# Reordering the first loads of a spectral-mixing kernel: filters side by side behind x, weights and the second batch held back

## The chip, the cores and the metric

The kernel runs on one NeuronCore of a Trainium2 chip. The metric is the device time of one execution in microseconds (us), as the median of several runs. "The trace" is the record of one profiled execution; its times count from the start of that execution's span.

## The reference, cut to what matters

```python
def _attn_ref(x, filt_r, filt_i):            # x: (8, 3008, 256), filters: (1505, 256)
    X = np.fft.rfft(x, axis=1)
    Y = X * (filt_r + 1j * filt_i)[None, :, :]
    return np.fft.irfft(Y, n=x.shape[1], axis=1)

def _moe_ref(x, w_in, w_out, beta):          # w_in: (256, 2048), w_out: (2048, 256)
    h = x @ w_in
    g = h * (1.0 / (1.0 + np.exp(-beta * h)))
    return g @ w_out
```

Each of the eight batches is transformed along its 3008 rows, multiplied by a filter, and transformed back. All rows then go through a two-layer network (the FFN).

## The kernel before

The transform is done as small matmuls. The first batch has a stage of its own, about 50 us long, in which little can be overlapped. From the second batch on, the transform of the next batch is hidden under the FFN of the current one. So what matters here is when the first FFN matmul (`hps`) can start.

The first stage needs, in this order: x of batch 0 (forward transform, `first1`), the filters (`product`), and then, for the FFN, w_in, x of batch 1 and w_out. All are loads from memory, issued from two queues:

```python
    x_cur = load_x(0, X_FIRST)                       # POOL queue, six pieces, f32 to bf16
    nc.sync.dma_start(bt[:], ...)                    # SP queue
    mark = dpool.tile([1, D], BF16, name="mark", tag="mark")
    nc.sync.dma_start(mark[:], x_cur[:1, 2 * JG, :]) # SP waits here for x's fifth piece
    ...
    FG = ((0, KG), (KG, KG), (2 * KG, 2 * KG))       # three groups: a quarter, a quarter, a half
    for k0, n in FG:
        load_filter(fr_sb, filt_r, 0, k0, n, nc.sync)   # each: rows upwards, rows downwards
    for k0, n in FG:
        load_filter(fr_sb, filt_i, M, k0, n, gp)        # gp is POOL
    ws = [load_wout(i * WG, WG) for i in range(2)]      # SP, behind filt_r
    ... # five small POOL instructions
    for h in range(WI):
        gp.dma_start(win_sb[:, :, fs], moe_w_in[:, fs]...)   # POOL, behind filt_i
    ... # tables; first1(0) to first1(7) use up x_cur
    xs[1] = load_x(1, X_WHOLE)                       # POOL, into the buffer of x_cur
    ...
    def beta_columns():
        bps = hpsum.tile([P, NFB], F32, name="bps", tag="hps")
        id_f = setup.tile([NFB, NFB], F32, name="id_f", tag="id_f")
        gp.tensor_copy(id_f[:], ident[:NFB, :NFB])   # POOL
        nc.tensor.transpose(bps[:], bt[:], id_f[:])  # TensorE
        nc.vector.tensor_copy(beta_sb[:], bps[:])    # VectorE
    ...
    for i in range(NK // 2 + FLAG):
        if i < NK // 2:
            product(i)        # two matmul pairs, then two VectorE products with fr_sb
        ...
        if i == 3:
            t2_more(1, nc.vector)
            beta_columns()
        ...
        if i >= FLAG:
            inverse3(i - FLAG)
```

`mark` is a copy whose only purpose is to make SP wait: the filt_r loads stand behind it in SP's program and start only when the named piece of x has landed (in the trace the piece landed at 10.78, the mark was issued at 10.80, the first filt_r load at 11.12).

There are twelve pairs of products; `pb_t` and `qb_t` are the two results of a pair. `beta_columns` turns a small vector into columns with a TensorE transpose (`bps`). For it POOL copies `id_f`, a 16x16 unit matrix. The filter's rows upwards are long runs; the rows downwards come as 1 KB pieces (sizes as in the trace's DMA records).

Of the kernel before, what the change touches and what calls it, by code (L numbers as in the profile page):

```python
# [9 lines left out]
P = 128  # L10
# [3 lines left out]
F32 = mybir.dt.float32  # L14
# [10 lines left out]
M = 64  # L25
H = M // 2
NK = 24
J = 32
KG = 6
NG = NK // KG  # L30
JG = 8
# [5 lines left out]
def kernel(  # L37
# [10 lines left out]
    nc = tc.nc  # L48
# [9 lines left out]
    NP = 2 * N1  # L58
# [26 lines left out]
    fr_sb = consts.tile([P, NK, D], F32, name="fr_sb", tag="fr_sb")  # L85
# [17 lines left out]
    def evac(dst, src, on_act, scale=None):  # L103
        if on_act:
            nc.scalar.activation(dst, src, ACT.Copy, scale=1.0 if scale is None else scale)  # L105
        elif scale is None:
            nc.vector.tensor_copy(dst, src)  # L107
        else:
            nc.vector.tensor_scalar_mul(dst, src, scale)  # L109

    def load_x(b, parts):
        t = xpool.tile([NP, J, D], BF16, name="xg", tag="xg")
        xv = x[b].rearrange("(p j) d -> p j d", j=J)
        for p0, p1, j0, j1 in parts:
            nc.gpsimd.dma_start(t[p0:p1, j0:j1, :], xv[p0:p1, j0:j1, :])  # L115
        return t


    X_WHOLE = [(0, 80, 0, J), (80, NP, 0, J)]
    X_FIRST = [(0, 80, 0, JG), (80, NP, 0, JG), (0, 80, JG, 2 * JG), (80, NP, JG, J)]  # L120
    X_FIRST += [(0, 80, g * JG, (g + 1) * JG) for g in range(2, NJG)]

# [29 lines left out]
    setup = sp.enter_context(tc.tile_pool(name="setup", bufs=1))  # L152
# [25 lines left out]
    def warm(n, cols=512):  # L178
        for _ in range(n):
            nc.tensor.matmul(pw[0][:, :cols], lhsT=wz[:, :P], rhs=wz[:, :cols], start=True, stop=True)  # L180
# [4 lines left out]
    nc.gpsimd.iota(ic[:], pattern=[[1, P]], base=0, channel_multiplier=0)  # L185
    x_cur = load_x(0, X_FIRST)
    bt = setup.tile([NFB, P], F32, name="bt", tag="bt")
    nc.sync.dma_start(bt[:], moe_beta.rearrange("(fb fp) -> fb fp", fp=P))

    mark = dpool.tile([1, D], BF16, name="mark", tag="mark")  # L190
    nc.sync.dma_start(mark[:], x_cur[:1, 2 * JG, :])

    gp = nc.gpsimd
    ip_f = small("ip_f")
# [18 lines left out]
    gp.tensor_tensor(keep[:], keep[:], m_p[:], ALU.mult)  # L213
    gp.tensor_scalar(keep[:], keep[:], 0.5, None, ALU.is_gt)

    WI = 2
    for h in range(WI):
        fs = slice(h * FF // WI, (h + 1) * FF // WI)
        gp.dma_start(win_sb[:, :, fs], moe_w_in[:, fs].rearrange("(dc p) f -> p dc f", p=P))
# [84 lines left out]
    def first1(i, on_act):  # L304
        for dc in range(NDC):
            if dc:
                ps = opsum.tile([P, 4, P], F32, name="psa", tag="acc")
            else:
                ps = fpsum.tile([P, 4, P], F32, name="psa", tag="f")
            for e in range(4):  # L310
                nc.tensor.matmul(
                    ps[:, e, :KP],
                    lhsT=x_cur[:, 4 * i + e, dc * P : (dc + 1) * P],
                    rhs=t1b[:],
                    start=True,
                    stop=True,
                )
            evac(
                a_t[:, dc, :, 4 * i : 4 * i + 4, :].rearrange("p k j a -> p j k a"),
                ps[:, :, :KP].rearrange("p j (k a) -> p j k a", a=4),  # L320
                on_act[dc],
            )
# [15 lines left out]
    first1(6, (True, True))  # L338
    warm(2)
    first1(7, (False, True))  # L340
    xs = {}
    if B > 1:
        xs[1] = load_x(1, X_WHOLE)



# [327 lines left out]
    def ux(b):  # L674
        def go():
            xs[b] = load_x(b, X_WHOLE)

# [147 lines left out]
```

## Time and profile before

| what | before |
|---|---|
| time, median of the first three runs | 810.47 us |
| span of the trace | 806.2 us |
| TensorE busy, whole span | 97% |
| VectorE's waits for filt_r | 6.45 and 7.32 us |
| first product, last product (start) | 22.92, 47.84 us |
| first `hps` | 53.19 us |

Busy time by stretches of ten us; the columns are the stretch, its length, busy us (and count) of TensorE, of its weight loads, of VectorE, ScalarE and POOL, then the granted TensorE clock, the DMA engines' busy share (it passes 1 where packets overlap, as with the 1.13 here) and GB/s:

```profile
20.00:30.00 10.00, 5.74 (x53) 5.08 (x53) 6.97 (x15) 4.97 (x9) 0.59 (x3) 0.66 1.13 235
30.00:40.00 10.00, 4.99 (x72) 4.51 (x70) 2.42 (x5) 5.69 (x9) 0.34 (x2) 0.95 1.02 213
40.00:50.00 10.00, 7.64 (x76) 6.49 (x76) 7.80 (x14) 3.85 (x8) 7.24 (x8) 0.70 0.26 80
```

No compute engine is full there, and the granted clock drops to a mean of 0.66 and 0.70 in two of the stretches, but the DMA engines are full until 40 us (1.13 and 1.02). The waits from 10 to 60 us (total, times, longest) name the reason:

```profile
DVE pb_t L424 <- DMA fr_sb<-in_filt_r_dram: 13.8, 2, 7.3
PE ps2q L415 <- DVE qb_t L424: 11.5, 2, 6.2
```

The first line is the cause and the second its echo: TensorE waits for buffers that VectorE has not read. VectorE's timeline gives the two places (start, length, instruction, and in brackets the idle time before it and what ended it), TensorE's timeline the first FFN matmul:

```profile
22.92 0.69 DVE L424 TENSOR_TENSOR pb_t<-ps,fr_sb 128x512 bf16<-128x512 f32 x1 [6.45 <-DMA fr_sb<-in_filt_r_dram]
...
39.87 0.69 DVE L424 TENSOR_TENSOR pb_t<-ps,fr_sb 128x512 bf16<-128x512 f32 x1 [7.32 <-DMA fr_sb<-in_filt_r_dram]
...
47.84 0.68 DVE L424 TENSOR_TENSOR qb_t<-ps2q,fr_sb 128x512 bf16<-128x512 f32 x1
...
53.19 1.02 PE L747 MATMUL hps<-y,win_sb 128*128 128x512 bf16 x4
```

From the first to the last product 24.92 us pass; without the second wait, 17.60. When the loads were issued, from the timelines of the SP and POOL queues:

```profile
10.80 0.27 SPq L191 DMA_DIRECT2D mark<-xg  x1
11.12 0.33 SPq L127 DMA_DIRECT2D fr_sb<-in_filt_r_dram  x1
...
12.43 1.56 POOL L219 DMA_DIRECT2D win_sb<-in_moe_w_in_dram  x2
18.37 1.11 POOL L115 DMA_DIRECT2D xg<-in_x_dram  x2 [4.38 <-PE pb L371]
19.47 0.19 POOL L389 CAST id_f<-ident 16x16 f32<-16x16 bf16 x1
```

So w_in and the second batch are issued 27 and 21 us before filt_r's last group lands (39.8), and share the engines with it: from 28 to 34 us their queue moved 83 packets and filt_r's 83.

### The profile page before, as it was taken

What the parts mean: (1) busy time and instruction counts of PE and PEld (TensorE: products, weight loads), DVE (VectorE), ACT (ScalarE), POOL (GpSimd) and SP (SyncE); (2) the same over time, 40 slices, a digit from 0 to 9 for tenths busy, and PEclk for the clock granted to TensorE, in tenths of its full rate; (3) what the DMA queues carried; (4) which work ended last, traced back from release to release, by engine and by line L of the source; (5) the groups of instructions that cost most, each with busy time, mean ns of one, the idle gap of its engine ahead of it and who ended that gap; (6) DMA issues with size and microseconds to landing.
All of it is one profiled execution on the core that took longest, in us unless ns stands there. A gap on an engine that the chain in (4) does not pass through costs nothing.

```text
span 806.2 us, 15374 instructions
## 1 busy us (share of the span) xinstructions
PE 780.4 (97%) x6101; PEld 550.8 (68%) x6101; DVE 398.7 (49%) x644; ACT 599.1 (74%) x920; POOL 142.2 (18%) x146
## 2 busy tenths in 40 slices
PE   7589999999999999999999999999999999999997
PEld 4466766766667766777667766787666776776665
DVE  6474964565636745275553746446463670500100
ACT  6557787787677876778667886678767788677776
POOL 6070430231002400033001320023100240000000
PEclk9889999999999999999999999999999999999999
DMA  8949379412941249311781118701291124110101
GB/s 182 225 109 221 119 163 216 148 67 100 206 151 42 96 113 193 122 57 67 177 201 59 51 62 208 202 27 69 102 229 47 48 90 111 41 53 28 53 27 52
DMA packets 84209, 91.43 MB, mean 113 GB/s; under 512 B 3563, under 2 KB 75004, under 8 KB 83338
## 3 DMA queue, kind: packets, MB, share of 16 engines
q1 hardware_dynamic: 79930, 72.11, 30.2%
q0 software_dynamic: 2272, 14.94, 9.8%
q10 hardware_dynamic: 1936, 3.41, 2.0%
q8 instruction: 47, 0.77, 0.4%
q14 instruction: 24, 0.20, 0.1%
HBM read 57.16 MB, written 46.66 MB: 129 GB/s over the span
## 4 chain that ended last, share of the span: by engine, by line
PE 88%; DMA 5%; DVE 3%; issue 2%; ACT 1%; POOL 0%; SPq 0%; ACTq 0%; DVEq 0%; POOLq 0%
PE acc L775 39%; PE hps L747 38%; DMA fr_sb<-in_filt_r_dram 3%; PE ps L550 3%; PE ps L498 2%; PE ps L572 2%; PE ps L599 2%; DVE ost L107 1%; DMA d<-a 1%; DMA xg<-in_x_dram 1%; DVE p_t L582 0%; ACT gT L756 0%; DMA a<-d 0%; DVE q_t L583 0%; DVE q_t L586 0%
## 5 line engine op out<-in xcount | busy, mean ns | idle before, releaser
L756 ACT ACTIVATE gT<-hps,beta_sb 128x512 bf16<-128x512 f32 x752 | 516.7, 687 | 177.6 <-PE hps L747 168.5
L775 PE MATMUL acc<-wout_sb,gT 128*128 128x256 bf16 x3008 | 455.1, 272 | 1.5 <-DVE ost L107 0.3
L747 PE MATMUL hps<-y,win_sb 128*128 128x512 bf16 (+7 forms) x1728 | 447.6, 351 | 0.0
L775 PEld LDWEIGHTS <-gT 128*128 128x128 bf16 x3008 | 285.7, 98 | 132.5 <-issue 4.2
L747 PEld LDWEIGHTS <-win_sb 128*128 128x128 bf16 x1728 | 164.8, 98 | 24.8 <-issue 0.5
L589 POOL TENSOR_TENSOR v_t<-p_t,q_t 128x512 bf16<-128x512 f32 x84 | 106.6, 1269 | 379.1 <-DVE q_t L586 371.6
L107 DVE COPY ost<-acc 128x512 f32<-128x512 f32 x87 | 56.1, 683 | 195.7 <-PE acc L775 189.1
L107 DVE CAST a<-ps 96x512 bf16<-96x512 f32 x96 | 65.9, 686 | 84.4 <-PE ps L550 82.8
L109 DVE TENSOR_SCALAR y<-ps 128x376 bf16<-128x376 f32 x118 | 64.4, 548 | 61.6 <-PE ps L498 61.4
L582 DVE TENSOR_TENSOR p_t<-ps,fr_sb 128x512 f32<-128x512 f32 x84 | 58.1, 691 | 33.3 <-PE ps L572 31.9
L586 DVE TENSOR_TENSOR q_t<-ps,fi_sb 64x512 f32<-64x512 f32 x84 | 58.2, 693 | 1.2
L583 DVE SCALAR_TENSOR_TENSOR q_t<-ps,fi_sb 64x512 f32<-64x512 f32 x84 | 57.4, 683 | 1.1
L498 PEld LDWEIGHTS <-zz 96*128 96x128 bf16 x512 | 35.5, 98 | 29.6 <-DVE q_t L586 0.8
L105 ACT ACTIVATE z<-ps 128x512 bf16<-128x512 f32 x84 | 49.5, 590 | 0.6 <-PE hps L747 0.4
L550 PE MATMUL ps<-xg,t 94*96 94x512 bf16 x112 | 41.9, 381 | 0.8 <-DVE a L107 0.7
L498 PE MATMUL ps<-t,zz 96*128 96x94 bf16 x448 | 36.8, 205 | 0.0
L572 PE MATMUL ps<-a,t 128*128 128x256 bf16 x168 | 32.1, 273 | 1.0 <-DMA a<-d 1.0
L599 PE MATMUL ps<-v_t,t 128*128 128x256 bf16 x168 | 32.1, 273 | 0.3 <-DVE q_t L586 0.2
L115 POOL DMA_DIRECT2D xg<-in_x_dram x20 | 10.9, 550 | 121.2 <-PE acc L775 97.7
L572 PEld LDWEIGHTS <-t 128*128 128x128 bf16 x168 | 15.9, 98 | 15.9 <-issue 1.3
L550 PEld LDWEIGHTS <-t 94*96 94x96 bf16 x112 | 13.8, 123 | 13.0 <-issue 1.3
L599 PEld LDWEIGHTS <-t 128*128 128x128 bf16 x168 | 15.4, 98 | 8.1 <-DVE q_t L586 0.5
(112 smaller groups left out, 207.5 us busy)
## 6 DMA issues: line engine op xcount, KB each, us to landing
out_dram<-ost SPq DMA_DIRECT2D x40, 512.0 KB, 2.9
d<-a SPq DMA_DIRECT2D x28, 384.0 KB, 11.1
a<-d SPq DMA_DIRECT2D x28, 384.0 KB, 4.3
d<-z SPq DMA_DIRECT2D x28, 384.0 KB, 3.4
zz<-d SPq DMA_DIRECT2D x28, 384.0 KB, 6.6
xg<-in_x_dram POOLq DMA_DIRECT2D x7, 1280.0 KB, 10.4
out_dram<-ost SPq DMA_DIRECT2D x20, 128.0 KB, 2.4
ws<-in_moe_w_out_dram SPq DMA_DIRECT2D x4, 512.0 KB
```

The costliest lines, as they stand in the source:

```text
L107: nc.vector.tensor_copy(dst, src)
L109: nc.vector.tensor_scalar_mul(dst, src, scale)
L498: nc.tensor.matmul(ps[:, e, :NP], lhsT=zz[:, jj + e, dc * P : (dc + 1) * P], rhs=tab[:], start=True, stop=True,)
L550: nc.tensor.matmul(ps[:KP], lhsT=t1[:], rhs=s["x"][:, 2 * i : 2 * i + 2, :], start=True, stop=True)
L572: nc.tensor.matmul(ps[:, e, :], lhsT=t2[:, k0 + e, 3:5, :].rearrange("p c k -> p (c k)"), rhs=s["a2"][g][:, kk + e, :], start=True, stop=True,
L582: nc.vector.tensor_tensor(p_t[:], ps[:], fr_sb[:, k0 : k0 + 2, :], ALU.mult)
L586: nc.vector.tensor_tensor(q_t[:M], ps[M:P], fi_sb[M:P, k0 : k0 + 2, :], ALU.mult)
L589: nc.gpsimd.tensor_tensor(v_t[:], p_t[:], q_t[:], ALU.add)
L599: nc.tensor.matmul(ps[:, e, :], lhsT=t3[:, k0 + e, :], rhs=v_t[:, e, :], start=True, stop=True)
L747: nc.tensor.matmul(hps[:, pos - t0 : pos - t0 + ln], lhsT=win_sb[:, dc, fb * P : (fb + 1) * P], rhs=ys[b][:, dc, n0 : n0 + ln], start=(dc ...
L756: nc.scalar.activation(gT[:, :tn], hps[:, :tn], ACT.Silu, scale=beta_sb[:, fb : fb + 1])
L775: nc.tensor.matmul(acc[tb // 2][:, tb % 2, :], lhsT=gT[:, tb * P : (tb + 1) * P], rhs=wout_sb[:, fb, :], start=(fb == 0 and tb % 2 == 0), ...
```

## The change

Its intent: order the loads by need. Both filters should come side by side close behind x, and w_in and the second batch only when the first half of both filters has landed. The whole diff:

```diff
+    X_HALVES = [(0, 80, 0, J // 2), (80, NP, 0, J // 2), (0, 80, J // 2, J), (80, NP, J // 2, J)]
...
-    nc.sync.dma_start(mark[:], x_cur[:1, 2 * JG, :])
+    nc.sync.dma_start(mark[:], x_cur[:1, JG, :])
...
+    held = setup.tile([P, 1], F32, name="held", tag="held")
+    for p0 in (H, M + H):
+        gp.tensor_copy(held[p0 : p0 + H], fr_sb[p0 : p0 + H, 2 * KG - 1, :1])
     WI = 2
     for h in range(WI):          # the w_in loads on POOL
...
-        xs[1] = load_x(1, X_WHOLE)
+        xs[1] = load_x(1, X_HALVES)
```

It has three parts: the mark waits for x's third piece instead of the fifth ("the earlier mark"); two tiny POOL copies read the second group of both filters and thereby hold POOL until these have landed ("the hold"); and the second batch comes in four pieces instead of two ("the halves").

## The prediction

> **What bounds the kernel now.** TensorE is busy 97% of the span (page, part 1), but not in the first 50 us: in 20-30, 30-40 and 40-50 us it is busy 5.7, 5.0 and 7.6 of 10 (busy time by stretches), with its clock granted at half for 22.1-28.9 and 39.0-46.0. This first-batch stage is set by VectorE's 24 filter products (pb_t, qb_t, 0.68 us each). VectorE waits for DMA fr_sb<-in_filt_r_dram twice, 13.8 us in all (waits): 6.45 us before the first product (22.92) and 7.32 us before the seventh pair (39.87). The products end at 48.5; the first FFN matmul (hps) starts at 53.2.
>
> Why filt_r is late: its queue (SP) starts only when the mark copy sees x's fifth piece (10.8), and its first packets move at about 16.5. Landings by semaphore: third x piece 8.5, fifth 10.9; filt_i groups 14.1, 16.0, 20.3; filt_r groups 22.9, 26.7, 39.9. The last group took 11 us more because it shared the engines with w_in and with the second batch. From 28 to 36 us the DMA records show 16 KB packets (1.23 us) and 1 KB packets (0.07 us) nearly one for one, so the filter got 0.16 MB in 8 us against 1.39 MB.[...]
>
> **What the change does.**
> 1. mark waits for x's third piece: SP's filter issue moves from 11.1 to about 8.8. filt_r then shares with the end of x and with filt_i.
> 2. Two tiny POOL copies (about 0.2 us each) wait for the second groups of both filters. POOL issues w_in (two issues, 0.78 us each) and the second batch behind them, so they move from 12.4 and 18.4 to about 23 and 24.5. The last filter group then meets only a tail of w_in's 2 KB packets.
> 3. The second batch comes in four pieces with 8 KB packets, 0.55 us of POOL per issue.
>
> No arithmetic moves. DMA is already full from 4 to 39 us, so total load time is conserved: w_out and batch 2 should still land near 41-42.
>
> **Cost on the critical path** (estimates from the above). First filter group lands at about 19 instead of 22.9: -3.9. The products then need 18.3 us of VectorE time with its small waits (25.6 less 7.32). Group 2 is in time, and the third lands near 29, before its need: -7.3. New wait, +2: beta_columns' id_f copy on POOL now stands behind the hold and six issues, about 27 instead of 19.5; the bps transpose and beta_sb (VectorE, in order) would like it at about 25. Products end near 39.5, hps starts near 44. Batch 2 and w_out land just in time, and the rest, TensorE at 97%, shifts as a block. Saving about 9 us, off 810.5.
>
> **Prediction:** 801.3 us, range 797.5 to 805. Faster by over 2%: 0.03; within 2%: 0.95; slower: 0.02.
>
> **What would show it.** VectorE's wait before the first pb_t about 2.5 us, before the seventh pair under 1 us; a new wait of about 2 us at beta_sb or bps, released by POOL id_f; hps at 42-46.
>
> **What would make it wrong.** filt_r no sooner despite the earlier issue; POOL held longer, so the id_f wait reaches 4 us; w_out's 1 KB packets starved by batch 2 until after 44, which would stall the first acc matmuls; x's last pieces delayed enough to push the first stage.

## The result, and the profile after

| what | before | after |
|---|---|---|
| time, median | 809.76 us (4 runs) | 801.85 us (4 runs) |
| ratio | | 0.990 (95%: 0.9878 to 0.9922) |
| span of the trace | 806.2 us | 800.1 us |
| first wait of VectorE for filt_r | 6.45 us | 4.51 us |
| second wait | 7.32 us | none |
| first product, last product (start) | 22.92, 47.84 | 20.79, 41.84 |
| first `hps` | 53.19 us | 47.20 us |

A ratio is the mean time of one kernel's fast runs over that of the other's of the same rounds, so it is not quite the ratio of the medians. A second set of runs, later, gave 802.05 against 808.38 us, ratio 0.9924. The saving is therefore 6 to 8 us. In the two traces it is 6.1 us of span, and `hps` starts 6.0 us sooner: the rest of the kernel shifted as a block.

The stretches of ten us after the change, columns as above:

```profile
20.00:30.00 10.00, 4.66 (x39) 3.84 (x39) 6.50 (x14) 4.58 (x8) 5.30 (x13) 0.65 1.09 241
30.00:40.00 10.00, 9.75 (x117) 9.02 (x116) 8.23 (x15) 7.15 (x13) 2.79 (x4) 0.84 1.07 215
40.00:50.00 10.00, 9.10 (x98) 6.27 (x97) 6.37 (x11) 6.79 (x12) 9.76 (x11) 1.00 0.51 132
```

The stretch from 30 to 40 us is now filled with work, that from 20 to 30 is emptier than before (4.66 us of TensorE instead of 5.74). The waits from 10 to 60 us show a new chain:

```profile
POOL held L220 <- DMA fr_sb<-in_filt_r_dram: 10.8, 1, 10.8
...
DVE pb_t L430 <- DMA fr_sb<-in_filt_r_dram: 4.5, 1, 4.5
...
PE bps L396 <- POOL id_f L395: 3.2, 1, 3.2
...
DVE beta_sb L398 <- PE bps L396: 1.5, 1, 1.5
```

VectorE waits for filt_r once, not twice. But POOL stands in the hold for 10.8 us, and TensorE then waits 3.2 us for a 16x16 copy on POOL. VectorE's timeline and the first `hps`:

```profile
20.79 0.69 DVE L430 TENSOR_TENSOR pb_t<-ps,fr_sb 128x512 bf16<-128x512 f32 x1 [4.51 <-DMA fr_sb<-in_filt_r_dram]
...
28.43 0.17 DVE L398 COPY beta_sb<-bps 128x16 f32<-128x16 f32 x1 [1.49 <-PE bps L396]
29.82 0.69 DVE L430 TENSOR_TENSOR pb_t<-ps,fr_sb 128x512 bf16<-128x512 f32 x1 [1.22 <-PE ps L421]
...
32.80 0.69 DVE L430 TENSOR_TENSOR pb_t<-ps,fr_sb 128x512 bf16<-128x512 f32 x1 [1.70 <-PE ps L421]
...
34.47 0.68 DVE L430 TENSOR_TENSOR pb_t<-ps,fr_sb 128x512 bf16<-128x512 f32 x1
...
41.84 0.68 DVE L430 TENSOR_TENSOR qb_t<-ps2q,fr_sb 128x512 bf16<-128x512 f32 x1
...
47.20 1.02 PE L753 MATMUL hps<-y,win_sb 128*128 128x512 bf16 x4
```

The seventh pair (34.47) has no wait. First to last product takes 21.05 us, 3.45 more than the 17.60 of before without its wait. The account closes: 2.13 us from the earlier first product, plus 7.32 from the lost second wait, minus 3.45, is 6.00. The queues show why the copy is late:

```profile
9.43 0.27 SPq L192 DMA_DIRECT2D mark<-xg  x1
9.74 0.33 SPq L128 DMA_DIRECT2D fr_sb<-in_filt_r_dram  x1
...
23.47 0.42 POOL L220 COPY held<-fr_sb 32x1 f32<-32x1 f32 x2 [10.76 <-DMA fr_sb<-in_filt_r_dram]
24.00 1.56 POOL L224 DMA_DIRECT2D win_sb<-in_moe_w_in_dram  x2
25.55 2.27 POOL L115 DMA_DIRECT2D xg<-in_x_dram  x4
27.86 0.19 POOL L395 CAST id_f<-ident 16x16 f32<-16x16 bf16 x1
```

id_f stands behind the hold and 3.8 us of DMA issues. When the parts of each load had all landed (us, from the trace's completion records):

```
                           before               after
x, third piece             8.4                  9.4
filt_i, groups 1, 2, 3     14.0  15.9  20.1     14.3  15.9  21.1
filt_r, groups 1, 2, 3     22.8  26.6  39.8     20.7  23.3  27.1
w_in                       30.6                 34.7
second batch               38.7                 41.9
w_out, parts 1, 2          41.0  42.4           28.4  30.0
```

w_out gained most, although nothing was done to it. It stands behind filt_r on the SP queue, and after the hold that queue had the engines almost to itself from about 20.5 to 27 us (1180 packets, 1.47 MB, began to move there, and none of the POOL queue).

### The profile page after: what moved, and what is told of

Same layout as the page of the kernel before. It is cut to its first block, busy times and chain, and to the rows that moved or that the text cites. A ratio compares the mean times of both kernels' runs of the same rounds, so it can differ in the third digit from the quotient of the medians.

```text
span 800.1 us, 15381 instructions
## 1 busy us (share of the span) xinstructions
PE 780.2 (98%) x6101; PEld 550.2 (69%) x6101; DVE 398.8 (50%) x644; ACT 599.1 (75%) x920; POOL 144.0 (18%) x150
## 3 DMA queue, kind: packets, MB, share of 16 engines
q10 hardware_dynamic: 1936, 3.41, 2.0%
## 4 chain that ended last, share of the span: by engine, by line
PE 89%; DMA 4%; DVE 3%; issue 2%; ACT 1%; POOL 1%; SPq 0%; ACTq 0%; DVEq 0%; POOLq 0%
PE acc L781 39%; PE hps L753 38%; PE ps L556 3%; PE ps L504 2%; PE ps L578 2%; PE ps L605 2%; DMA fr_sb<-in_filt_r_dram 2%; DVE ost L107 1%; DMA d<-a 1%; DMA xg<-in_x_dram 1%; PE psz L440 0%; POOL xg L115 0%; DVE p_t L588 0%; DMA a<-d 0%; DVE q_t L589 0%
## 5 line engine op out<-in xcount | busy, mean ns | idle before, releaser
L588 DVE TENSOR_TENSOR p_t<-ps,fr_sb 128x512 f32<-128x512 f32 x84 | 58.1, 692 | 33.6 <-PE ps L578 32.2
L504 PEld LDWEIGHTS <-zz 96*128 96x128 bf16 x512 | 35.4, 98 | 29.7 <-DVE q_t L592 0.8
L556 PE MATMUL ps<-xg,t 94*96 94x512 bf16 x112 | 41.9, 381 | 0.3 <-DVE zz L107 0.2
## 6 DMA issues: line engine op xcount, KB each, us to landing
d<-a SPq DMA_DIRECT2D x28, 384.0 KB, 11.3
xg<-in_x_dram POOLq DMA_DIRECT2D x6, 1280.0 KB, 10.2
```

Source lines behind the costliest of these rows:

```text
L504: nc.tensor.matmul(ps[:, e, :NP], lhsT=zz[:, jj + e, dc * P : (dc + 1) * P], rhs=tab[:], start=True, stop=True,)
L556: nc.tensor.matmul(ps[:KP], lhsT=t1[:], rhs=s["x"][:, 2 * i : 2 * i + 2, :], start=True, stop=True)
L588: nc.vector.tensor_tensor(p_t[:], ps[:], fr_sb[:, k0 : k0 + 2, :], ALU.mult)
```

## The experiments

The theory after the result was: (A) the hold removes the second wait; the earlier mark shortens the first; id_f's place behind the hold takes back part of both. The rivals were that one part carries everything, or that the growth of the products' time has another cause. All kernels below gave correct results.

### Each part alone

Only the mark:

```diff
-    nc.sync.dma_start(mark[:], x_cur[:1, 2 * JG, :])
+    nc.sync.dma_start(mark[:], x_cur[:1, JG, :])
```

> The kernel before with only the mark copy moved from x's fifth to its third piece; w_in and the second batch are not held. Theory A (three separate gains; the hold alone cures the third filter group): the filter issue on SP starts near 9.4 us instead of 10.8, the first wait of VectorE for filt_r falls from 6.5 to about 4.5 us, the second (seventh pair) stays large, 4 to 7 us[...]. Total gain 2 to 5 us, about 806.5. Rival B (what matters is the earlier start, the hold adds little): gain 7 us or more, and the second wait under 1 us.

Measured: 806.27 us against 808.35, ratio 0.9977 (0.9956 to 0.9998). The first wait was 4.51 us, but the second grew to 8.88 us: the last filter group still landed at 39.0, with the end of the second batch. The gain of 2 us is just clear of the noise and at the lower end of what A gave, because the second wait came out longer than its 4 to 7 us; B fell.

Only the hold (the `held` tile and its two copies, nothing else):

> The kernel before with only the hold on POOL. Theory A: the second wait of 7.3 us goes, the first stays near 6 us, and a new wait for POOL's id_f copy of about 3.4 us of VectorE time appears, so the gain is about 4 us (806). Rival B: gain under 1.5 us. Rival C (the hold carries the whole change): gain of 7 us or more.

Measured: 801.23 us, ratio 0.9915 (0.990 to 0.993). Rival C was right, and the size that A gave was wrong: the hold alone is worth as much as the whole change. The second wait was gone. The new wait for id_f was there, but only 1.2 us long at TensorE, and VectorE lost 0.53 and 0.26 us to it, probably because the products started late (22.99) and POOL had two batch issues fewer to make before id_f (two took 1.11 us in the kernel before, four 2.27 in the changed one).

Only the halves:

```diff
-        xs[1] = load_x(1, X_WHOLE)
+        xs[1] = load_x(1, X_HALVES)
```

> The kernel before with only the second batch loaded in four pieces, 8 KB instead of 16 KB packets, nothing held. If the engines alternate between the queues packet by packet, then halving the packets of the batch doubles the filter's packets in the same time: of some 390 packets of the last filter part about 160 landed in 28 to 36 us, about 90 more would, and the second wait falls from 7.3 to about 5 us, total gain about 2 us. If the engines share by bytes or by time, nothing changes (within 0.5 us).

Measured: 808.0 us, ratio 0.9997; the second wait was 7.91 us. The expected gain did not come. But the packet counts moved as expected. These are packets of the POOL queue and of the SP queue, counted in the trace's DMA records:

```
us          before (16 KB)    halves (8 KB)    fourths (4 KB, below)
28 to 30      34 :  35          80 :  74          107 : 107
30 to 32      28 :  28          65 :  65          107 : 114
32 to 34      21 :  20          46 :  46          119 : 114
filter's last packet lands    39.8      40.2      35.4
second batch's last lands     38.7      40.3      39.0
```

In these stretches the two queues moved nearly as many packets as each other at all three sizes (83 and 83, 191 and 185, 333 and 335 in the 6 us), and the halves did give the filter 2.2 times as many packets (185 instead of 83). What the expectation forgot is the count: a third group has 384 packets of 1 KB, a mean of 24 for each of the 16 engines on the profile's page, and at 8 KB the batch has 188, a mean of 12. Even when the batch's first packet moved, at 27.8, 275 of the filter's were still to come. So the batch ended first in the kernel before (38.7 against 39.8), and with the halves both ended together (40.3 and 40.2).

### The same idea with packets that suffice

The kernel before, with the batch in eight pieces of 4 KB packets (376 packets, a mean of 24 for each engine); id_f is moved ahead so that the extra issues do no other harm (these lines are left out here):

```diff
+    X_FOURTHS = [(p0, p1, g * JG, (g + 1) * JG) for g in range(NJG) for p0, p1 in ((0, 80), (80, NP))]
-        xs[1] = load_x(1, X_WHOLE)
+        xs[1] = load_x(1, X_FOURTHS)
```

> The kernel before (no hold, mark at the fifth piece) with the second batch in eight pieces of 4 KB packets; id_f is moved ahead so that the extra issues on POOL do no other harm. With 8 KB packets the filter moved 2.2 times as many packets from 28 to 34 us, yet its last group still landed with the end of the batch, 40.2: per engine some 24 filter packets stood against 12 of the batch, so one for one cannot finish it before the batch ends. With 4 KB packets it is about 24 against 24: the last filter packets land before the batch's last, near 36 to 37.5, second wait 4 to 5.5 us, total 805 to 806. If packet counts do not decide it: second wait over 7 us as before.

Measured: 804.96 us against 808.05, ratio 0.9958 (0.9938 to 0.9978). The last filter packet landed at 35.4, 3.6 us before the batch's last, and the second wait fell to 2.45 us:

```profile
35.49 0.69 DVE L425 TENSOR_TENSOR pb_t<-ps,fr_sb 128x512 bf16<-128x512 f32 x1 [2.45 <-DMA fr_sb<-in_filt_r_dram]
```

The nearly equal counts (107 and 107, 107 and 114, 119 and 114 in the table) held at this size, too. They show how many packets each queue moved in a stretch, not in which order an engine took them; that the engines alternate packet by packet was not shown. The early id_f cannot be the reason for the gain: in the kernel before, the bps transpose did not wait for id_f (copied at 19.47, used at 27.76). Cutting a large load of low urgency into smaller packets made this kernel faster: beside 4 KB packets the filter moved 335 packets from 28 to 34 us, beside 16 KB packets 83.

### id_f ahead of the hold

All parts of the change, and:

```diff
     keep = ...
+    gp.tensor_copy(id_f[:], ident[:NFB, :NFB])      # taken out of beta_columns
     held = ...
```

> The changed kernel with the id_f copy on POOL moved ahead of the hold. Theory A (the time of VectorE from the first product to the last grew from 18.3 to 21.7 us because the bps transpose waits 3.2 us for id_f behind the hold and the six DMA issues): TensorE's wait for POOL disappears, first product to last takes 18.3 to 19 us, first hps near 44 us instead of 47.2, total 798.5 to 799.5. Rival D (the growth comes from ScalarE's table work or from TensorE's half clock colliding with products that now start earlier): products still take over 20.5 us and the total falls by less than 1.2 us against the changed kernel.

Measured: 797.17 us, ratio 0.9862 (0.9845 to 0.9878) against the same runs of before as the mark-only, hold-only and halves-only kernels. TensorE's wait for id_f was gone, first to last product took 16.29 us instead of 21.05, and `hps` started at 43.28. Theory A holds; D fell.

```profile
26.34 0.28 PE L396 MATMUL bps<-id_f,bt 16*128 16x16 f32 x1
...
37.92 0.68 DVE L430 TENSOR_TENSOR qb_t<-ps2q,fr_sb 128x512 bf16<-128x512 f32 x1
...
43.28 1.02 PE L753 MATMUL hps<-y,win_sb 128*128 128x512 bf16 x4
```

The gain is 3 to 5 us of time, depending on which of its two sets the changed kernel is taken from. The products' stretch shrank by 4.8 us, more than the 3.2 us for which TensorE had stood still. A likely reason is the clock. After the change TensorE idled 3.35 us before 22.1 and again 3.2 us for id_f, and the trace grants it half clock from 23.0 to 33.3; the waits of 1.22 and 1.70 us at 29.82 and 32.80 fall into that time. With id_f early, half clock lasted 3.4 us.

The half-clock stretches in the first 60 us of the traces quoted here are 3.4, 6.8 or 10.2 us long. In the changed kernel TensorE was busy 0.91 us of the 3.41 before half clock began. In the first two thirds of the 10.2 us, with the wait for id_f between them, it was busy 1.86 and 1.76 us of 3.41; in the last it was busy throughout, and then the full clock came back. With id_f early it was busy 4.95 us from 25 to 30 (1.89 in the changed kernel), at a mean clock of 0.84 instead of 0.50. So less idle time and less half clock went together here; what decides the grant was not shown.

What the clock costs is seen in the repeats below: the same two waits were 1.22 and 1.70 us again in the second traces of the changed and the hold-only kernel, both at half clock, though VectorE had waited 2.00 and 0.71 us for the transpose itself. In the first hold-only trace, at full clock from 28.2, they were 0.53 and 0.26. That puts about 2 us on the clock, as an estimate (2.92 less 0.79); no run changes the clock alone.

### What the earlier mark and the halves are worth beside the hold

Hold and early mark, batch in two pieces:

```diff
-        xs[1] = load_x(1, X_HALVES)
+        xs[1] = load_x(1, X_WHOLE)
```

> The changed kernel with the second batch again in two pieces: hold and earlier mark remain. Theory A' (the earlier mark starts the products 2 us sooner, and the wait for POOL's id_f takes it back, because id_f stands behind the hold and the DMA issues): two issues fewer put id_f 1.1 us sooner, VectorE's stall between products 3 and 4 shrinks by 1 to 2 us, hps at 45.3 to 46.3 instead of 47.2, total 800 to 801. Rival (the four pieces do no harm): hps within 0.4 us of 47.2.

Measured: 798.5 us, but from 797.21 to 802.13, ratio 0.9886 (0.9858 to 0.9913). In its trace id_f was awaited for 2.2 us instead of 3.2 and `hps` started at 43.06, earlier than expected; but x's third piece happened to land at 7.7 in that trace, 1.7 us sooner than in the changed kernel's. The direction is as expected, the size is not settled.

Hold and early id_f, no earlier mark, no halves:

> Hold and early id_f alone: the mark copy at x's fifth piece and the batch in two pieces, as before. If the earlier mark is worth what the first wait showed (first product at about 21 instead of 23 us) once id_f is out of the way, this is 1.3 to 2.2 us slower than the run with all parts and early id_f: hps near 45, total about 799. Rival (the mark is worth nothing): the same as that run within 0.5 us. In the hold-only run products took 17.9 us with the late id_f, so early id_f should gain here under 0.7 us.

Measured: 799.38 us, ratio 0.9890 (0.9875 to 0.9905), against 0.9862 (0.9845 to 0.9878) with all parts and early id_f, timed in another set; the intervals just touch. So the earlier mark and the halves together are worth about 2 us when id_f is early, as expected; `hps` was at 44.71. Early id_f gained about 2 us over hold-only, more than the 0.7 expected from hold-only's one trace; the second trace below, with a longer wait, fits better.

Since these differences are small, the changed kernel and the hold-only kernel were run again, five rounds on one chip:

> The changed kernel once more, unaltered, beside the hold-only kernel on one chip, because the two were timed in different rounds (0.990 and 0.9915 of before) and single traces disagree by 1.5 us on when x's third piece lands. Theory (the earlier mark and the four pieces are worth nothing net while id_f is late; early id_f made them worth about 2 us): this and hold-only agree within 0.8 us. Rival (they are worth 1.5 us or more here, too): this is at least 1.5 us faster. The bps transpose should wait 2.5 to 4 us for id_f.

> The hold-only kernel once more, unaltered, beside the changed kernel. Theory: within 0.8 us of it, near 0.991 of before; the bps transpose waits 1 to 2 us for id_f, VectorE's products take 17.5 to 18.5 us from first to last, and start 1 to 3 us later than in the changed kernel.

Measured: the changed kernel 802.05 us, ratio 0.9924 (0.9904 to 0.9945); hold-only 801.78 us, ratio 0.9909 (0.9891 to 0.9927). They are the same. While id_f is late, the earlier mark and the halves are worth nothing net. The two details expected of hold-only were wrong: in this trace its products started early, at 20.82 (in the changed kernel at 21.81), id_f was then awaited for 2.4 us, and the products took 20.62 us. That is instructive in itself. Of two traces of one kernel, hold-only, the one that started its products 2.2 us sooner started `hps` 1.2 us later (first product, the two waits for TensorE and `hps` of the first trace, then of the second):

```profile
22.99 0.69 DVE L427 TENSOR_TENSOR pb_t<-ps,fr_sb 128x512 bf16<-128x512 f32 x1 [4.50 <-DMA fr_sb<-in_filt_r_dram]
...
29.74 0.69 DVE L427 TENSOR_TENSOR pb_t<-ps,fr_sb 128x512 bf16<-128x512 f32 x1 [0.53 <-PE ps L418]
...
31.30 0.69 DVE L427 TENSOR_TENSOR pb_t<-ps,fr_sb 128x512 bf16<-128x512 f32 x1 [0.26 <-PE ps L418]
...
45.58 1.02 PE L750 MATMUL hps<-y,win_sb 128*128 128x512 bf16 x4
```

```profile
20.82 0.69 DVE L427 TENSOR_TENSOR pb_t<-ps,fr_sb 128x512 bf16<-128x512 f32 x1 [4.63 <-DMA fr_sb<-in_filt_r_dram]
...
29.07 0.69 DVE L427 TENSOR_TENSOR pb_t<-ps,fr_sb 128x512 bf16<-128x512 f32 x1 [1.22 <-PE ps L418]
...
32.06 0.69 DVE L427 TENSOR_TENSOR pb_t<-ps,fr_sb 128x512 bf16<-128x512 f32 x1 [1.70 <-PE ps L418]
...
46.80 1.02 PE L750 MATMUL hps<-y,win_sb 128*128 128x512 bf16 x4
```

Here the earlier start, which ran into the late id_f, gained nothing. In the second trace half clock lasted 10.2 us, in the first 3.4 us in this place.

### Why the first filter group is still late

With id_f early, the first wait of 4.9 us is the largest that is left. In the DMA records of the changed kernel, from 16 to 17 us, 17 packets of filt_i's third group (mean 11 KB) move beside 27 of filt_r's first group (mean 1.3 KB). Theory E takes the large packets beside it as the reason why the group lands late. So filt_i's third group was put behind the hold:

```diff
-    for k0, n in FG:
+    for k0, n in FG[:2]:
         load_filter(fr_sb, filt_i, M, k0, n, gp)
 ...
     held = ...                                  # the hold, as before
+    load_filter(fr_sb, filt_i, M, *FG[2], gp)
```

> All parts of the change, early id_f, and filt_i's third group issued after the hold, too. Theory E (the first group of filt_r, on the SP queue in 1 KB packets, lands late, at 20.7 to 21.5[...]): the first group lands at 17.5 to 19, the first wait falls from 4.9 to 1 to 2.5 us, the third groups land by 27 in time for the seventh pair, hps at 40.5 to 42 instead of 43.3, total 794.5 to 796. Rival F (the wait is the start-up time of SP's queue behind the backlog of x, or total bytes): first group no sooner than 20.5, total within 0.7 us of the run with early id_f.

Measured: filt_r's first group landed at 16.9 and the first wait fell to 0.91 us, so theory E's landing and wait came as expected. In this trace x's third piece landed early, at 8.15, which is part of it. Counted from that landing the group came 8.8 us later, against 11.3 to 11.9 us in the five traces with the earlier mark and three groups; so about 3 us are owed to the edit. It took filt_i's bytes away together with its large packets and does not tell the two apart, so theory E's reason was not shown by it. But the time was 799.05 us, ratio 0.9888: no better than 0.9862. The gain came back as a new wait, now for the other filter:

```profile
17.06 0.69 DVE L431 TENSOR_TENSOR pb_t<-ps,fr_sb 128x512 bf16<-128x512 f32 x1 [0.91 <-DMA fr_sb<-in_filt_r_dram]
...
30.80 0.69 DVE L431 TENSOR_TENSOR pb_t<-ps,fr_sb 128x512 bf16<-128x512 f32 x1 [3.65 <-DMA fr_sb<-in_filt_i_dram]
...
43.31 1.02 PE L754 MATMUL hps<-y,win_sb 128*128 128x512 bf16 x4
```

filt_i's third group landed at 30.5, behind filt_r's (23.6) and alongside w_out's two parts (24.9 and 31.7), which were first used at 33.6.

The next try keeps that order with four equal groups for both filters:

```diff
-    FG = ((0, KG), (KG, KG), (2 * KG, 2 * KG))
+    FG = ((0, KG), (KG, KG), (2 * KG, KG), (3 * KG, KG))
```

> The run with filt_i's third group behind the hold, with both filters in four equal groups, so that the seventh pair needs only a third group of half the size. There the first wait had shrunk from 4.9 to 0.9 us and a new wait of 3.65 us for filt_i had taken the gain back at the seventh pair. Theory: the third group of filt_i now lands near 25 to 26.5, wait at the seventh pair under 1 us, the fourth by 30, wait at the tenth pair under 1.5 us; hps near 40 to 41.5, total 794 to 796.5. Rival (VectorE's 18 us of products and the load are balanced, any order only moves the wait): waits at the seventh and tenth pair together over 3 us, total within 1 us of 798.

And, as its control, four equal groups without the third and fourth behind the hold:

> All parts, early id_f, filters in four equal groups, nothing of filt_i behind the hold. Packets of filt_i's second half are 6 KB instead of 12 KB. If the size of the packets that filt_r's first group alternates with sets when it lands, the first group lands 0.7 to 1.5 us sooner than the 20.7 to 21.5 of the runs with three groups (near 19.5 to 20.3), not as early as the 16.9 with the third group held. If not, it lands at 20.7 or later. Total 796 to 797.5.

Measured: 796.2 us (0.9846; 0.9829 to 0.9862) and 795.52 us (0.9838; 0.9819 to 0.9858) against 808.55. For four groups alone, filt_r's first group landed at 19.2, as expected of smaller packets (10.3 us after x's third piece, against 11.3 to 11.9: the packets' size alone gives about 1 of the 3 us above, an estimate from one trace), and VectorE then had no other wait for data: 16.15 us from first to last product, at full clock throughout.

```profile
19.33 0.69 DVE L430 TENSOR_TENSOR pb_t<-ps,fr_sb 128x512 bf16<-128x512 f32 x1 [3.02 <-DMA fr_sb<-in_filt_r_dram]
...
40.83 1.02 PE L753 MATMUL hps<-y,win_sb 128*128 128x512 bf16 x4
```

With the second half of filt_i behind the hold, the first product started 2.6 us sooner, at 16.77, but `hps` 0.7 us later:

```profile
29.01 0.69 DVE L432 TENSOR_TENSOR pb_t<-ps,fr_sb 128x512 bf16<-128x512 f32 x1 [1.85 <-PE pt L360]
...
41.52 1.02 PE L755 MATMUL hps<-y,win_sb 128*128 128x512 bf16 x4
```

The profile names a TensorE result as the releaser at 29.01, but VectorE had copied that result already; what had just landed, at 28.7, was filt_i's third group. The remaining 1.4 us come from small waits before, among them one for ScalarE's tables (0.27 us at 22.49). So the total came as expected, but the wait at the seventh pair did not, and the control shows that the total is owed to the four groups: holding half of filt_i back added nothing. From a first product at about 19 us on, a better place for one load was paid for by another. The kernel with four groups, early id_f and all parts of the change beats both the kernel before and the changed one.

Over all traces, `hps` and the span move together (from `hps` to the end it takes 752.6 to 753.7 us in all 14), so the rest of the kernel is a block. Seven of them:

```
kernel                       first product   first hps   span    time (ratio to before)
before                           22.92         53.19     806.2
mark only                        21.19         52.69     805.5   0.9977
fourths, early id_f              22.97         47.99     801.2   0.9958
change                           20.79         47.20     800.1   0.9900
hold only                        22.99         45.58     798.3   0.9915
change, early id_f               21.63         43.28     796.9   0.9862
change, early id_f, 4 groups     19.33         40.83     794.3   0.9838
```

## Why the prediction was right or wrong

The total was right: 801.85 us measured (802.05 in the second set) against 801.3, inside the range, and within 2%. The saving is 6 to 8 us, though, not 9. That the total fits so closely is partly luck: the kernel before, put at 810.5, gave 808.05 to 808.55 in the later sets, and this offset the saving that was put too high.

- **The second wait, "-7.3": right.** The hold removed it. The third filter group landed at 27.1 (predicted 29) and the wait was zero. Hold-only shows that this is the whole net gain of the change; the prediction gave it 7.3 of 9.2 us.
- **The first wait, "-3.9": too large.** The first group landed at 20.7 instead of about 19, and the first product started 2.1 us sooner. Over the traces the mean first product is at 20.9 us with the earlier mark and three groups (19.2 to 21.8; five traces, that with filt_i's third group held back is left out) and at 22.4 with the late one (20.8 to 23.1; six traces), a gain of 1.5 us. The prediction moved the landing more than the issue. It missed that filt_r's 1 KB packets then meet the 12 KB packets of filt_i's third group (27 and 17 packets from 16 to 17 us); holding those back brought the landing to 16.9. It had the one-for-one count in hand and applied it to the second batch only.
- **The new wait, "+2": right in place, too small.** id_f ran at 27.86 (predicted 27) and was the releaser that the prediction named. Its cost was 3.45 us in the first trace and 4.6 in the second (22.19 less 17.60). In the first trace VectorE's wait for the transpose itself was only 1.49 us. The part that was not foreseen is the slow restart of TensorE behind it, at half clock: 2.92 us, where the kernel before had 0.99 us of such waits. Early id_f showed the whole to be removable.
- **"hps at 42-46": wrong, 47.20**, as the sum of these two terms.
- **Batch 2 and w_out "near 41-42": half right.** The batch landed at 41.9, w_out's first parts at 28.4 and 30.0. Total load time was nearly conserved (the last of these loads landed at 42.4 before, at 41.9 after), but the order within it changed, and w_out moved ahead. It caused no stall.
- **"The rest shifts as a block": right**, to 0.1 us.
- **Four pieces for the batch** were costed only as POOL time. Alone they changed nothing (0.9997).

## What to carry to other kernels

When two queues share the DMA engines, count packets as well as bytes: here, from 28 to 34 us of the kernel before, each queue moved 83 packets, but the filter's were 0.085 MB and the other's 1.12. Try holding the other load back (0.9915 here) or cutting it until it has at least as many packets (0.9958 here). When an engine is made to wait on purpose, list everything that follows on that engine in program order; a copy of 16x16 behind such a hold cost 3 to 5 us here. And a load that arrives sooner is worth only what the next wait behind it leaves: the first wait fell from 4.9 to 0.91 us here, and a new one of 3.65 took the gain back.

## What else the traces show

- In the kernel before, from 28 to 36 us, the filter's queue, in 1 KB packets, got 0.17 MB against 1.37 MB on POOL's, nearly all in 16 KB packets, and what helped was the number of packets (last filter packet at 39.8, 40.2 and 35.4 us for 16, 8 and 4 KB).
- SP's first load, issued at 0.73 us by an instruction of 0.40, moved at 1.76. With x and filt_i still moving on POOL's queue it took far longer: the 512-byte mark copy was issued at 10.80 and its packet moved at 16.5; after the change, at 9.43 and 14.7. That POOL's backlog is the reason was not tested.
- The landing of the same loads varies from run to run: x's third piece, loaded by identical code, landed at 7.7 to 10.0 us in these traces. A few tenths of a per cent should not be read from one trace.
